# Sliding-window attention into a gated feed-forward layer: another order for the tail rows' loads, the first score tiles, batch 1's steps, the later q and k jobs and the last output tile

## The chip, the cores and the metric

The kernel runs on one core of one Trainium2 chip. The time is the device time of one execution in microseconds (us); five executions of the kernel before gave 329.77, 330.66, 330.7, 331.74 and 332.5, and their median, 330.7 us, is the number to compare with. One execution was also recorded by the hardware profiler. It is the one of 331.74 us; the recorded span, from the first to the last instruction, is 330.0 us of it, and 1.7 us lie around the span. All instants below are us from the start of that span.

The engines are called PE (TensorE, the matrix engine; PEld is its weight load), ACT (ScalarE), DVE (VectorE), POOL (GpSimd) and SP (SyncE, which here only issues transfers).

## The reference, cut to what matters

```python
# q, k, v: 8 batches x 8 heads x 576 rows x 64, float32
scores = q @ k.T / 8
rel = pos[:, None] - pos[None, :]
mask = (rel >= 0) & (rel < 128)                 # each row sees itself and 127 rows before it
scores = where(mask, scores - slope[h] * abs(rel), -1e9)
attn = softmax(scores, axis=-1)
x = (attn @ v) put together to 4608 tokens x 512
h = x @ w_in                                    # 512 -> 2048
g = h * sigmoid(beta * h)
out = g @ w_out                                 # 2048 -> 512, float32
```

Attention is small and banded: a block of 128 keys meets only its own block of query rows and the next one. The two dense products of the second half are large: 4608 x 512 x 2048 each.

## The kernel before, in words

**Tiling.** A batch has 576 = 4 x 128 + 64 rows; the last 64 rows are its tail. Heads go in pairs p = 0..3. `SC(b, m, p)` makes a score tile of a pair, transposed (keys on the partitions): m = 0 holds key blocks 0 and 1, m = 1 holds key blocks 2, 3 and 4, of which block 4 is the tail. Its matmuls are at L285; in batches 0 and 1 two matmuls at L271 add the bias first and one ACT exponential follows (L293); in later batches four ACT exponentials (L298) and a DVE mask (L302) follow. `PV(b, qb, g)` multiplies the exponentials of four heads with v (L325, L329), and DVE divides by the row sums (L334, L335). `X(b, qb)` brings the result to the layout that the dense half reads, `XT`: for batches 0 to 2 by four PE transposes and a copy out of PSUM (L358; ACT for batches 0 and 2, DVE for batch 1), from batch 3 on by a transposing transfer from SP (L349). `HS(g, j)` is one of 16 slices of the first dense product for a group g of 512 tokens: four matmuls (L372), a tanh on ACT (L377) and a multiply on DVE into `gT` (L378). `OS(g, i, n)` is a quarter of the second product for 128 tokens (four matmuls, L388; quarter n reads slices 4n to 4n+3 of `gT`); after n = 3 the tile is scaled and stored. There are nine groups.

**How q, k and v come in.** All loads from DRAM are f32. For batches 0 to 2, `load_pair(b, p)` loads 512 rows of q and of k of two heads in runs of 1024 bytes (L109), and POOL casts them to bf16 (L113). `load_tail(b)` loads the tails of all heads in runs of 256 bytes (L95), and POOL casts them (L119). PE transposes them, `TP(b, p, i)` (i = 0 for q, 1 for k; L224) and `TT(b)` for the tail (L238), and ACT or DVE copies the result to `QK[b % 2]` (L229, L243). From batch 3 on, `load_qk(b, sb)` loads a block of 128 rows of q and of k in runs of 256 bytes (L95), POOL casts both (L129), and `TD(b, sb)` issues two transposing transfers from SP into `QK` (L248), one for q and one for k. v is loaded by SP and cast by POOL (L142) for batches 0 to 2, and loaded with a cast by POOL's own queue later (L137). W_in comes in four POOL transfers (L188) and W_out in four (L191), some of them tied to follow a certain cast.

**What sets the order.** PE's order is the program's order, written by hand. For SP and POOL this holds as well from the line with `steps, first = ...` on (L657): `merge` puts jobs (loads, casts, transposing transfers) between the attention steps by a due step. `first[b]` is the step at which batch b's scores begin: 26 for batch 3, 47 for batch 4, 70, 93 and 116 for the others. A q, k job of block sb is due at `first[b] - 25 + 4.6 * sb`, its cast 4.5 steps later and its `TD` 8.5 steps later. SP and POOL run their lists strictly in order; SP waits where a cast isn't done. `spread(moe, todo, lead, goals)` mixes dense items with attention steps: after each dense item it runs as many steps as the sum of their costs (1 or 2 each) allows, on a straight line that begins after `lead` items.

**PSUM.** Transposes, `PV` and `X` of batches 0 to 2 share two buffers (`psum_t`, tag "t"). `HS` has two. In batch 1 score tiles alternate between `psum_s` and `psum_y`, one buffer each.

**Batches 0 and 1 and the end.** Batch 0's steps are a written list (L586 to L609); batch 1's are `by_pair(1)`, seven `HS` items of group 0 between them (L640). The last group's items at L672 are 16 `HS` with the 13 open `OS` of the group before between the first 13 of them; then 16 `OS` follow at L685.

Of the kernel before, what the change touches and what calls it, by code (L numbers as in the profile page):

```python
# [17 lines left out]
def kernel(  # L18
# [98 lines left out]
    def load_tail(b):  # L117
        for i, src in enumerate((q, k)):
            nc.gpsimd.tensor_copy(  # L119
                out=tails[b % 2][0 : S - LM, i], in_=load_rows(src, b, NQB - 1)  # L120
            )
# [37 lines left out]
        nc.gpsimd.memset(VS[i][64:P, 4, :, :], 0.0)  # L159
        nc.gpsimd.memset(VS[i][:, :, :, D : D + 1], 1.0)  # L160
    nc.scalar.dma_start(out=bflat[:], in_=moe_beta.rearrange("(j p) -> j p", p=P))
    load_pair(0, 0)
    load_pair(0, 1)
    load_tail(0)
    load_pair(0, 2)
    load_pair(0, 3)
    for h in range(H):
        nc.scalar.mul(sident[:, h, :], ident[:], slopes[h] / qscale)

# [171 lines left out]
    def X(b, qb):  # L341
        nq = ROWS[qb]
        xnv = xns.pop((b, qb))[:].rearrange("p h d -> p (h d)")
        tok0 = (b * S + P * qb) % XTR
        n1 = min(nq, XTR - tok0)
        parts = [(tok0, 0, n1)] + ([(0, n1, nq)] if n1 < nq else [])
        if b >= NTE:
            for at, r0, r1 in parts:
                nc.sync.dma_start_transpose(out=XT[:, :, at : at + r1 - r0], in_=xnv[r0:r1, :])  # L349
            return  # L350
        xt = psum_t.tile([P, NDM, P], BF16, name="xt", tag="t")
        for c in range(NDM):
            nc.tensor.transpose(
                out=xt[:, c, :], in_=xnv[:, c * P : (c + 1) * P], identity=ident[:]
            )
        copy = nc.vector.tensor_copy if b == 1 else nc.scalar.copy
        for at, r0, r1 in parts:
            copy(out=XT[:, :, at : at + r1 - r0], in_=xt[:, :, r0:r1])  # L358

# [64 lines left out]

    cost = {}

    def spread(moe, todo, lead, goals):
        sums = [0]  # L430
        for f in todo:
            sums.append(sums[-1] + cost.get(f, 0))
        goals = [(m, sums[n]) for m, n in goals]
        m0, w0, k = lead, 0, 0
        slope = None
        for i, it in enumerate(moe):
            flush()
            it()
            while goals and (slope is None or i + 1 >= m1):

                if slope is not None:
                    m0, w0 = m1, w1
                    goals = [g for g in goals if g[0] > m0]
                    if not goals:
                        break
                slope, m1, w1 = max(((w - w0) / (m - m0), m, w) for m, w in goals)
            w = w0 + slope * (i + 1 - m0)
            while k < len(todo) and (sums[k] + sums[k + 1]) / 2 <= min(w, w1):
                todo[k]()
                k += 1  # L450
        for f in todo[k:]:
            f()

    def step(f, c):
        cost[f] = c
        return f

    def tp(b, p, i):
        return step(lambda: TP(b, p, i), 1)

    def tt(b):
        return step(lambda: TT(b), 1)

    def sc(b, m, p):
        def f():
            pool = None
            if "y" in spare:
                pool = spare["y"][0]
                spare["y"].reverse()
            SC(b, m, p, pool)  # L470

        return step(f, 2)

    def pv(b, qb, g):
        return step(lambda: PV(b, qb, g), 1)

    def x(b, qb):
        f = step(lambda: X(b, qb), int(b < NTE))
        at[b, qb] = f
        if b >= NTE:  # L480
            lazy.append(f)
        return f
# [5 lines left out]
    def merge(steps, first):  # L488
        jobs = []

        def vals(b, sb, t0):
            casts = []
            jobs.append((t0, lambda: casts.append(load_v(b, sb))))
            if b < NTE:
                jobs.append((t0 + 4.5, lambda: casts.pop()()))

        for sb in range(NQB):
            vals(NTE - 1, sb, 1.5 * sb)
        for b in range(NTE, B):
            for sb in range(NQB):  # L500
                casts = []
                t0 = first[b] - 25 + 4.6 * sb
                jobs.append((t0, lambda b=b, sb=sb, c=casts: c.append(load_qk(b, sb))))
                jobs.append((t0 + 4.5, lambda c=casts: c.pop()()))
                jobs.append((t0 + 8.5, lambda b=b, sb=sb: TD(b, sb)))
                vals(b, sb, first[b] - 16 + 3 * sb)
        for i, f in enumerate(steps):
            if f in lazy:
                jobs.append((i + 2, f))
        jobs.sort(key=lambda j: j[0])  # L510
        out = []
        for i, f in enumerate(steps):
            while jobs and jobs[0][0] <= i:
                out.append(jobs.pop(0)[1])
            if f not in lazy:
                out.append(f)
        return out + [j[1] for j in jobs]

    def by_pair(b):
        return [  # L520
            tp(b, 0, 0), tp(b, 0, 1), tp(b, 1, 0), sc(b, 0, 0), tp(b, 1, 1), tp(b, 2, 0),
            sc(b, 0, 1), tp(b, 2, 1), tp(b, 3, 0), sc(b, 0, 2), tp(b, 3, 1), tt(b), pv(b, 0, 0),
            sc(b, 0, 3), pv(b, 1, 0), sc(b, 1, 0), pv(b, 0, 1), sc(b, 1, 1), pv(b, 1, 1),
            sc(b, 1, 2), x(b, 0), pv(b, 2, 0), sc(b, 1, 3), x(b, 1), pv(b, 3, 0), pv(b, 4, 0),
            pv(b, 2, 1),
        ]
# [30 lines left out]
    with tc.manual_schedule(engines={mybir.EngineType.PE}):  # L557
# [7 lines left out]
        for p in range(NP):  # L565
            c = load_pair(1, p, None if p else VS[0][0:1, NQB - 1, 0, 0:1])
            if p == 1:
                with tc.issue_after(c.ins):
                    load_w1(3)
                load_tail(1)  # L570
        for sb in range(NQB):
            c = load_v(1, sb)()
            if sb == 3:
# [3 lines left out]
        with tc.tile_pool(name="psum_x", bufs=2, space=bass.MemoryType.PSUM) as psum_x:  # L577
            pools = [psum_x, psum_s, psum_x]

            def sc0(m, p, fill=0):  # L580
                SC(0, m, p, pools[0], fill)
                pools.append(pools.pop(0))

            w = psum_t.tile([P, 512], F32, name="w", tag="t")
            idle(w[:], 9)
            TP(0, 0, 0)  # L586
            c = TP(0, 0, 1)
            with tc.issue_after(c.ins):
                late_consts()
            sc0(0, 0, 3)  # L590
            load_beta()
            TP(0, 1, 0)
            TP(0, 1, 1)
            sc0(0, 1, 2)
            TT(0)
            TP(0, 2, 0)
            sc0(1, 0, 1)
            TP(0, 2, 1)
            sc0(1, 1)
            TP(0, 3, 0)  # L600
            sc0(0, 2)
            TP(0, 3, 1)
            sc0(1, 2)
            PV(0, 0, 0)
            sc0(0, 3)
            PV(0, 1, 0)
            sc0(1, 3)
            for qb in (2, 3):
                PV(0, qb, 0)  # L609
# [22 lines left out]
            del spare["z"]  # L632
        for p in range(NP):
            load_pair(2, p)
            if p == 1:
                load_tail(2)

        with tc.tile_pool(name="psum_y", bufs=1, space=bass.MemoryType.PSUM) as psum_y:
            spare["y"] = [psum_s, psum_y]
            spread(h0[7:14], s1[2:-1], 0, [(7, len(s1) - 3)])  # L640
            del spare["y"]
        psum_o = ctx.enter_context(
            tc.tile_pool(name="psum_o", bufs=2, space=bass.MemoryType.PSUM))
# [13 lines left out]
        with tc.manual_schedule(engines={mybir.EngineType.SP, mybir.EngineType.Pool}):  # L657


            order = [(i, n) for i in range(4) for n in range(4)]  # L660

            def os(g, order):
                return [lambda i=i, n=n: OS(g, i, n) for i, n in order]

            todo = [[]]
            for f in merge(steps, first):
                if f in visits:
                    todo.append([])
                todo[-1].append(f)
            moe = [hs(1) + os(0, order[0:12]), os(0, order[12:]), os(1, order[0:3])]  # L670
            for g in range(2, NTG):
                o = os(g - 1, order[3:]) + (os(g, order[0:3]) if g < NTG - 1 else [])  # L672
                for j, h in enumerate(hs(g)):
                    moe[-1].append(h)
                    if j % 4 == 1:
                        moe.append([])
                    moe[-1] += o[j : j + 1]
            for n, m in enumerate(moe):
                r = todo[n] if n < len(todo) else []
                if n and r:  # L680
                    r.pop(0)()
                spread(m, r, 2 if n == 0 else 1, [(len(m) - (n == 0), len(r))])
            while stores:
                flush()
            for it in os(NTG - 1, order):  # L685
                it()


# [28 lines left out]
```

## Time and profile before

| quantity | value |
|---|---|
| median of five executions | 330.7 us |
| the profiled execution, and its span | 331.74 us, 330.0 us |
| PE busy | 313.8 us (95%) |
| ACT, DVE, POOL busy | 214.9, 190.7, 107.1 us |
| granted PE clock | full in every slice (only the first nine warm-up matmuls of 512 columns come 0.43 us apart, later ones 0.213 us) |
| q, k and v transfers issued by SP, median time to landing | 4.9 to 6.4 us |
| transposing transfers L248, median time to landing | 4.0 us |

PE's busy time counts every matmul to its modelled end, so a dense stretch reads as full. Where PE stands still it shows in the list of PE's waits, which names the instruction that waited and what released it. A transfer has two instants: the issue on its queue (SPq or POOLq rows) and the landing, after which its reader may start.

### The profile page before, as it was taken

The numbers are of one execution on the slowest core, as the hardware profiler recorded it, in microseconds if no ns is written. First come the engines' busy times: TensorE is split into PE (matmuls) and PEld (weight loads), VectorE is DVE, ScalarE is ACT, GpSimd is POOL, SyncE is SP. The second block draws the span as 40 slices with busy tenths as digits, with TensorE's granted clock in tenths as the row PEclk, the third lists the DMA queues.
The fourth block names the chain that finished last, engine by engine and source line by source line (L and its number), as shares of the span: only waits on it lengthen the run. The fifth ranks groups of instructions, "written<-read, shape, count | busy, mean of one in ns | idle before, by whom it ended". The sixth has DMA issues, their size and how long they took to land.

```text
span 330.0 us, 6155 instructions
## 1 busy us (share of the span) xinstructions
PE 313.8 (95%) x2238; PEld 154.0 (47%) x2280; DVE 190.7 (58%) x413; ACT 214.9 (65%) x416; POOL 107.1 (32%) x173
## 2 busy tenths in 40 slices
PE   8979798999998999999999999999999999999995
PEld 3444345544544544454445444444444444444442
DVE  7658458995445666666666666666665434433400
ACT  5757684887786777777777777777764444544411
POOL 7743583166553443433344235300000000010000
PEclk9999999999999999999999999999999999999999
DMA  7999999999999999999999899921122200001011
GB/s 183 257 186 253 223 231 237 187 203 184 203 208 180 185 217 174 189 186 201 176 171 184 159 193 193 176 64 51 48 71 68 57 32 32 32 34 64 33 66 64
DMA packets 138638, 48.26 MB, mean 146 GB/s; under 512 B 125664, under 2 KB 136176, under 8 KB 138608
## 3 DMA queue, kind: packets, MB, share of 16 engines
q1 hardware_dynamic: 108208, 32.19, 54.0%
q0 software_dynamic: 30224, 15.54, 30.9%
q8 instruction: 18, 0.29, 0.4%
q10 hardware_dynamic: 176, 0.14, 0.1%
q14 instruction: 12, 0.10, 0.1%
HBM read 36.71 MB, written 9.44 MB: 140 GB/s over the span
## 4 chain that ended last, share of the span: by engine, by line
PE 65%; DMA 21%; SPq 5%; POOL 2%; issue 2%; ACT 2%; DVE 1%; POOLq 0%
PE ops L388 32%; PE hps L372 27%; DMA fst<-in_v_dram 8%; DMA fst<-in_k_dram 7%; DMA fst<-in_q_dram 4%; PE sps L285 3%; SPq L248 2%; PE pv L329 2%; SPq L95 2%; PE pv L325 1%; DMA qkT<-bst 1%; SPq L109 1%; ACT pt L298 1%; POOL vs L142 1%; DVE gT L378 1%
## 5 line engine op out<-in xcount | busy, mean ns | idle before, releaser
L377 ACT ACTIVATE sig<-hps,beta_h 128x512 bf16<-128x512 f32 x144 | 99.8, 696 | 79.4 <-PE hps L372 60.9
L372 PE MATMUL hps<-XT,W 128*128 128x512 bf16 x554 | 144.1, 379 | 2.6 <-ACT XT L358 0.7
L388 PE MATMUL ops<-W,gT 128*128 128x512 bf16 x559 | 143.2, 379 | 1.4 <-issue 0.2
L378 DVE SCALAR_TENSOR_TENSOR gT<-sig,hps 128x512 bf16<-128x512 bf16 x144 | 98.3, 684 | 66.8 <-ACT sig L377 66.5
L388 PEld LDWEIGHTS <-gT 128*128 128x128 bf16 x576 | 53.9, 98 | 64.1 <-issue 2.1
L372 PEld LDWEIGHTS <-W 128*128 128x128 bf16 x576 | 51.1, 97 | 52.4 <-issue 3.8
L298 ACT ACTIVATE pt<-sps,bias 128x256 bf16<-128x256 f32 (+1 forms) x192 | 73.0, 494 | 3.7 <-PE sps L285 3.7
L129 POOL CAST bst<-fst 128x512 bf16<-128x512 f32 (+1 forms) x50 | 32.4, 650 | 77.2 <-DMA fst<-in_q_dram 60.8
L302 DVE TENSOR_TENSOR pt<-pt,mask 128x1024 bf16<-128x1024 bf16 x48 | 34.1, 711 | 36.2 <-ACT pt L298 36.1
L406 POOL DMA_DIRECT2D out_dram<-osb x32 | 17.9, 559 | 91.2 <-ACT osb L403 91.1
L335 DVE TENSOR_TENSOR xn<-pv,zs 128x256 bf16<-128x256 f32 (+1 forms) x80 | 33.7, 422 | 2.5
L403 ACT ACTIVATE osb<-ops 128x512 f32<-128x512 f32 x35 | 20.9, 598 | 15.3 <-PE ops L388 15.3
L329 PE MATMUL pv<-vs,pt 128*128 128x65 bf16 x320 | 28.6, 193 | 1.6 <-POOL vs L142 1.1
L329 PEld LDWEIGHTS <-pt 128*128 128x128 bf16 x320 | 21.7, 97 | 10.6 <-issue 0.8
L325 PE MATMUL pv<-vs,pt 128*128 128x65 bf16 x256 | 24.1, 193 | 0.7 <-DVE XT L358 0.5
L325 PEld LDWEIGHTS <-pt 128*128 128x128 bf16 x256 | 19.9, 98 | 8.0 <-issue 1.6
L285 PE MATMUL sps<-qkT 64*128 64x256 bf16 (+2 forms) x320 | 21.9, 251 | 1.5 <-DMA qkT<-bst 1.4
L137 POOL DMA_DIRECT2D vs<-in_v_dram x25 | 21.4, 855 | 0.6 <-issue 0.5
L285 PEld LDWEIGHTS <-qkT 64*128 64x128 bf16 x320 | 11.2, 94 | 20.5 <-issue 15.7
L113 POOL CAST bst<-fst 128x512 bf16<-128x512 f32 x24 | 14.6, 623 | 17.6 <-DMA fst<-in_q_dram 12.9
L334 DVE RECIPROCAL zs<-pv 128x4 f32<-128x4 f32 (+1 forms) x80 | 14.0, 176 | 10.9 <-PE pv L329 10.7
L293 ACT ACTIVATE pt<-sps 128x1024 bf16<-128x1024 f32 x16 | 16.4, 1024 | 6.0 <-PE sps L285 5.3
(49 smaller groups left out, 109.6 us busy)
## 6 DMA issues: line engine op xcount, KB each, us to landing
fst<-in_q_dram SPq DMA_DIRECT2D x32, 256.0 KB, 4.9
fst<-in_k_dram SPq DMA_DIRECT2D x32, 256.0 KB, 5.2
out_dram<-osb POOLq DMA_DIRECT2D x32, 256.0 KB, 3.6
fst<-in_v_dram SPq DMA_DIRECT2D x12, 256.0 KB, 6.4
vs<-in_v_dram POOLq DMA_DIRECT2D x20, 128.0 KB, 5.3
W<-in_moe_w_in_dram POOLq DMA_DIRECT2D x4, 512.0 KB, 7.2
W<-in_moe_w_out_dram POOLq DMA_DIRECT2D x4, 512.0 KB, 15.3
fst<-in_q_dram SPq DMA_DIRECT2D x8, 128.0 KB, 5.0
```

The costliest lines, as they stand in the source:

```text
L129: nc.gpsimd.tensor_copy(out=t[0 : ROWS[sb], i], in_=f)
L137: nc.gpsimd.dma_start(out=to, in_=v[b, :, P * sb : P * sb + ROWS[sb], :].rearrange("h p d -> p h d"))
L285: nc.tensor.matmul(o, lhsT=qk[64 * e : 64 * e + 64, 1, p, P * kb : P * kb + P], rhs=qk[64 * e : 64 * e + 64, 0, p, P * kb : P * kb + nq], ...
L298: nc.scalar.activation(out=pt[:, e, cols], in_=sps[e][:, cols], func=ACTF.Exp, scale=qscale, bias=bias[:, half, h : h + 1],)
L302: nc.vector.tensor_tensor(out=pt[:], in0=pt[:], in1=masks[m][:].rearrange("p (o c) -> p o c", o=1).broadcast_to([P, 2, 512]), op=ALU.mult,)
L325: nc.tensor.matmul(pv[:, hl, 0 : D + 1], lhsT=weights(b, qb - 1, h, 1), rhs=vs[:, qb - 1, h, 0 : D + 1], start=True, stop=False,)
L329: nc.tensor.matmul(pv[:, hl, 0 : D + 1], lhsT=weights(b, qb, h, 0), rhs=vs[:, qb, h, 0 : D + 1], start=qb == 0, stop=True,)
L335: nc.vector.tensor_tensor(out=xn[0:nq, 4 * g : 4 * g + 4, :], in0=pv[0:nq, :, 0:D], in1=zs[0:nq].broadcast_to([nq, 4, D]), op=ALU.mult,)
L372: nc.tensor.matmul(hps[:], lhsT=W1[:, c, bass.ts(j, P)], rhs=XT[:, c, c0 : c0 + TOKG], start=(c == 0), stop=(c == NDM - 1),)
L377: nc.scalar.activation(out=sig[:], in_=hps[:], func=ACTF.Tanh, scale=beta_h[:, j : j + 1])
L378: nc.vector.scalar_tensor_tensor(out=gts[g][:, j, :], in0=sig[:], scalar=1.0, in1=hps[:], op0=ALU.add, op1=ALU.mult)
L388: nc.tensor.matmul(ops_[:], lhsT=gT[:, j, i * P : i * P + P], rhs=W2[:, j, :], start=(j == 0), stop=(j == NFF - 1),)
```

## The change

Six edits. (1) In all of batches 0, 1 and 2 the tail's two loads and casts go behind the four pairs, where they stood between pairs 1 and 2. (2) In batch 0 the copies of `X` alternate between ACT (row blocks 0, 2, 4) and DVE (1, 3). (3) Batch 0's list makes the m = 0 tiles of all four pairs first, then the tail's transposes, then the m = 1 tiles. (4) Batch 1 gets a list of its own, in which score tiles come two at a time; `spread` runs the second of such a pair at once, and its `lead` for batch 1 is 1 in place of 0. (5) From batch 3 on a q, k job is due at `first[b] - 27.5 + 4.2 * sb`: 2.5 steps sooner for block 0 and 4.1 for block 4, with its cast and its `TD`. v's jobs keep their steps. (6) The first three quarters `OS(8, 0, 0..2)` of the last group stand behind its last three `HS` items, one behind each, as in the other groups.

```diff
-    load_pair(0, 0)
-    load_pair(0, 1)
+    for p in range(NP):
+        load_pair(0, p)
     load_tail(0)
-    load_pair(0, 2)
-    load_pair(0, 3)
...
-        copy = nc.vector.tensor_copy if b == 1 else nc.scalar.copy
+        copy = nc.vector.tensor_copy if b == 1 or b == 0 and qb % 2 else nc.scalar.copy
...
-    cost = {}
+    cost, second = {}, []
...
-            while k < len(todo) and (sums[k] + sums[k + 1]) / 2 <= min(w, w1):
+            while k < len(todo) and (
+                (sums[k] + sums[k + 1]) / 2 <= min(w, w1) or todo[k] in second
+            ):
...
+        if b == 1 and p % 2:
+            second.append(f)
         return step(f, 2)
...
-                t0 = first[b] - 25 + 4.6 * sb
+                t0 = first[b] - 27.5 + 4.2 * sb
...
     def by_pair(b):
+        if b == 1:
+
+            return [
+                tp(b, 0, 0), tp(b, 0, 1), tp(b, 1, 0), tp(b, 1, 1), tp(b, 2, 0), sc(b, 0, 0),
+                sc(b, 0, 1), tp(b, 2, 1), tp(b, 3, 0), tp(b, 3, 1), tt(b), sc(b, 0, 2),
+                sc(b, 0, 3), pv(b, 0, 0), pv(b, 1, 0), sc(b, 1, 0), sc(b, 1, 1), pv(b, 0, 1),
+                pv(b, 1, 1), sc(b, 1, 2), sc(b, 1, 3), x(b, 0), pv(b, 2, 0), x(b, 1),
+                pv(b, 3, 0), pv(b, 4, 0), pv(b, 2, 1),
+            ]
...
-                load_tail(1)
+        load_tail(1)
...
+            TP(0, 2, 0)
+            TP(0, 2, 1)
+            sc0(0, 2, 2)
+            TP(0, 3, 0)
+            TP(0, 3, 1)
+            sc0(0, 3)
             TT(0)
-            TP(0, 2, 0)
-            sc0(1, 0, 1)
-            TP(0, 2, 1)
+            sc0(1, 0)
             sc0(1, 1)
-            TP(0, 3, 0)
-            sc0(0, 2)
-            TP(0, 3, 1)
+            PV(0, 0, 0)
             sc0(1, 2)
-            PV(0, 0, 0)
-            sc0(0, 3)
             PV(0, 1, 0)
             sc0(1, 3)
...
-            if p == 1:
-                load_tail(2)
+        load_tail(2)
...
-            spread(h0[7:14], s1[2:-1], 0, [(7, len(s1) - 3)])
+            spread(h0[7:14], s1[2:-1], 1, [(7, len(s1) - 3)])
...
-                o = os(g - 1, order[3:]) + (os(g, order[0:3]) if g < NTG - 1 else [])
+                o = os(g - 1, order[3:]) + os(g, order[0:3])
...
-            for it in os(NTG - 1, order):
+            for it in os(NTG - 1, order[3:]):
```

## The prediction

> **What bounds the kernel now.** I read the page first (busy shares and the 40 slices):
>
> ```profile
> PE 313.8 (95%) x2238; PEld 154.0 (47%) x2280; DVE 190.7 (58%) x413; ACT 214.9 (65%) x416; POOL 107.1 (32%) x173
> ...
> PE   8979798999998999999999999999999999999995
> ...
> DMA  7999999999999999999999899921122200001011
> ```
>
> PE is the bound from about 100 us on, and no edit removes PE work, so only PE's pauses can be won: slices 1 to 7 and one later. The DMA row is full for two thirds of the span: early, a transfer's place in line matters as much as PE's order. PE's waits over the whole span, second:
>
> ```profile
> PE tps L224 <- POOL bst L113: 2.0, 1, 2.0
> PE sps L285 <- DMA qkT<-bst: 1.4, 1, 1.4
> ...
> PE pv L329 <- POOL vs L142: 1.1, 1, 1.1
> PE hps L372 <- ACT XT L358: 0.7, 1, 0.7
> PE hps L372 <- DVE gT L378: 0.6, 1, 0.6
> ```
>
> Each is one event. PE's timeline places them at 32.8, 98.5, 17.6, 22.4 and 310.5. Counted from matmul start to start, less the 0.213 us that a 512-column matmul takes in dense stretches, the second is 1.54 and the last 0.80. The third view is the chain of waits around the second:
>
> ```profile
> 93.51 0.62 POOL bst L129
> 94.14 1.30 SPq L248
> ...
> 95.53 4.31 DMA qkT<-bst
> ...
> 99.89 0.51 PE sps L285 x10
> ```
>
> PE reached SC(3,1,0) at 98.23 and stood until the k half of TD(3,4) landed at 99.84. Is that a late issue, or a full DMA? The DMA view of 64 to 100 us in 40 slices:
>
> ```profile
> DMA  6388999999999999929999999999999159999996
> ```
>
> Full, but for the start and two gaps. So TD(3,4) lands when the work ahead of it is through. That work starts with W_in, W_out and batches 1 and 2's loads, gated by v casts, not by PE's progress. It follows that PE's clock is reset at 99.84: whatever edits 1 to 4 win before that is spent waiting there, and whatever they lose is forgiven up to 1.5 us. This is the core of the forecast.
>
> [...] v's POOL load issued at 94.62 lands at 99.64, between the two halves of TD(3,4) (99.04 and 99.84). [...] batch 0's pairs (1024-byte runs) land 0.7 to 0.8 us apart, its tails, half the bytes in 256-byte runs, 0.9 us. [...]
>
> **Edits 1, 2, 3: batch 0.** PE's wait at 17.6 ends with v block 3's cast (18.00 to 18.62), whose load lands at 17.95. The ten q, k loads before it are the same, in another order, so the cast stays. New order up to there: pair 2's casts come about 1 us sooner, pair 3's end at 11.1 (12.7 before), the tail's at 12.7. With 0.69 us per DVE copy the m = 0 tiles end near 14.1, TT near 14.6, and four m = 1 tiles of 0.95 us with two PVs near 18.3: 0.3 us before v. Nothing won; the one more filler matmul (0.2 us) is hidden by that wait, and costs itself if v comes sooner. X's four ACT copies take 20.47 to 23.0 in a row. With two on DVE (0.42 us) block 1's copy stands ahead of block 3's reciprocal and multiply (0.18 and 0.42), so the last copy ends at 23.0 to 23.3: 0 to +0.2.
>
> **Edits 1, 4: batch 1.** TP(1,2,0) waits because POOL casts the tail first:
>
> ```profile
> 33.01 1.18 POOL L119 CAST tail<-fst 64x512 bf16<-64x512 f32 x2
> 34.12 1.17 POOL L113 CAST bst<-fst 128x512 bf16<-128x512 f32 x2
> ...
> 34.79 0.40 PE L224 MATMUL tps<-ident,bst 128*128 128x128 bf16 x4 [2.00 <-POOL bst L113]
> ```
>
> With the tail last, pair 2's q is cast from 33.01 to 33.63 and PE goes on at 33.7: 1.1 us won. What is late next: three TPs and TT now follow one another on two PSUM buffers. The third waits for the ACT copy of the first, which stands behind an exponential (1.02) and a tanh (0.69): about 1.1 us lost near 37; before, TT and PV lost 0.7 there. After h13, x, pv, x, pv, pv, pv come in a row on the same buffers; DVE's copies (0.42) and pairs (0.6) pace them as they did (0.67 + 0.32). By this count h14 comes at 51.1, before 51.2. It rests on DVE taking what is ready first, as at 44.43, where a reciprocal precedes the gT of an earlier slice; in strict program order I get 53.5. So PE's shift at 54 us lies between -0.2 and +2.3, and I take -0.1. All of it meets 99.84.
>
> **Edit 5: batch 3.** With the due steps written out, SP's list up to TD(3,4) holds the same transfers in both kernels (five v, seven q, k pairs, eight TDs); only the pairs of blocks 2, 3, 4 each move ahead of one TD. The same issues, the same bytes: no gain from SP. On POOL, v block 0 of batch 4 (step 31) stood ahead of the casts of q, k block 1 (31.1), now behind them (28.2). Those casts end at 98.1, so that load, which occupied the DMA from 97.5 to 99.3, drops behind TD(3,4). Its price is the spacing of such loads, 1.0 to 1.3 us. Bounds: 0, if the DMA fills otherwise, to 1.6, from where TD(3,4)'s own least time to landing (2.5 us, the shortest of any L248) binds. I take 1.1: PE goes on at 98.8 in place of 99.89, **-1.1**. On the way, SC(3,0,0) at 86.62 needs TD(3,2)'s q half (landed 86.19). It is now behind block 4's pair (0.66 + 0.69 of SP, 1.3 us of DMA), but ahead of two v loads that follow later casts (-2.6 us of DMA); SP's issue then binds, 86 to 87: at most 0.4 us, forgiven at 98.8. v and k casts of batch 2 swap places by two casts (1.2 us); PV(2,0,0) runs at 71, 4 us after v's cast.
>
> **Edit 5: batch 4.** The next first score tile and the transfer it needs, from the timelines of PE and SP:
>
> ```profile
> 115.88 0.61 PE L285 MATMUL sps<-qkT 64*128 64x256 bf16 x8
> ```
>
> ```profile
> 106.66 4.19 SPq L248 DMA_TRANSPOSE qkT<-bst  x2
> ```
>
> TD(4,2)'s q half took 7.8 us to land, at 114.5: 1.4 us of slack. PE now arrives at 114.8. SP's list before TD(4,2) gets block 4's pair in addition: 0.63 + 0.62 us of issue, 1.3 us of DMA; against that the DMA's empty slice near 106 (0.8 us). I get 115.0, bounds 113.5 and 118.4: **+0.3**. Batches 5 to 7 have slack of 3.3 to 5.2 us, and XT is read some 30 us after it lands.
>
> **Edit 6: the end.**
>
> ```profile
> 308.64 1.89 PE L372 MATMUL hps<-XT,W 128*128 128x512 bf16 x8
> ...
> 311.16 1.02 PE L372 MATMUL hps<-XT,W 128*128 128x512 bf16 x4 [0.63 <-DVE gT L378]
> ```
>
> Three HS in a row on two PSUM buffers lose 0.80. With an OS between (0.86 us) each buffer has 1.73 us and the loss goes, as in the earlier rows. But OS(8,0,3) now follows h15 by one OS. h15 starts at 312.1, its gT is ready 2.55 us later (1.06 to tanh, 0.72, 0.72), at 314.65; the fourth matmul of that OS would come at 314.45. Loss 0.2 (bounds 0 and 0.9, if the whole OS waits). **-0.6.**
>
> **Sum.** -1.1 + 0.3 - 0.6 = -1.4: the profiled execution goes from 331.74 to 330.3. The median shown is 330.7, 1.0 lower; I take the same difference: 329.3 us.
>
> **Rivals.** (a) TD(3,4) lands where it did, since the order of the same bytes moves nothing, or batch 1 loses 2.3 us and PE itself comes at 100: only the end is won, -0.6 to -0.5, 330.1. For it: the equal lists. Against: v's load ahead of it. (b) The DMA gains more, because casts done sooner let SP issue TDs without a pause (it waited 4.0 us on L129 casts from 75 to 105), and PE's early gain counts: -1.5 - 0.5 - 0.6 = -2.6, 328.1. Against: those pauses were filled by DMA work. (c) Slower: TD(4,2) becomes the bound. Batch 4's first v loads, dropped behind TD(3,4), fall into its way (two of 1.3 us) with block 4's pair (1.3): it lands at 118.4, PE waits 3.6 us: -1.1 + 3.6 - 0.6 = +1.9, 332.6. It decides from a landing after 116.5 on, 2.0 us later than before.
>
> **How the numbers follow.** A measurement of this kernel can tell about 0.5%, 1.65 us: faster is below 329.05, slower above 332.35. My forecast (own range 328.5 to 330.1) gets 0.45, of which 0.2 is faster; (b) 0.20, faster; (a) 0.20, of which 0.02 faster, the rest same; (c) 0.15, slower. That makes 0.42, 0.43 and 0.15. The range 327.8 to 332.0 leaves out the far ends of (b) and most of (c).
>
> **What would show it.** Right: PE's wait on the tps of pair 2 falls from 2.0 to about 1; a wait on qkT stays near 98 us, ended by TD(3,4), although PE came there at its time or sooner; batch 4's first score tile waits little; no HS wait at 310, a short OS wait at 314. Wrong: no wait on qkT at all with PE ahead by over 2 us; waits on qkT near 86 or 115 of over 1 us; new waits near 50 us of over 2 us in all.

## The result, and the profile after

The change makes the kernel slower. The median is 335.67 us over 44 executions, against 331.64 us over 79 executions of the kernel before on the same chips. The ratio is 1.0067, with a 95% interval from 1.0050 to 1.0085; it compares the executions of each kernel that lie within 1.5% of its own fastest, which is why it is smaller than the quotient of the medians, 1.0122. The prediction, 329.3 us and most likely faster or equal, was wrong.

The profiled execution of the kernel after took 338.19 us (span 336.2 us), one of the longer ones. Its main losses are named below and looked for again in the experiments. In the kernel after, most line numbers are two lower than before: L370 and L386 are the matmuls of `HS` and `OS` (before L372, L388), L283 those of the score tiles, L246 `TD` and L347 `X`. From the page, its span and the rows of PE and of PE's granted clock in the 40 slices (8.4 us each):

```profile
span 336.2 us, 6162 instructions
...
PE   7889888999799995999999999999999999999995
...
PEclk9999999999999999799999999999999999999999
```

PE has a hole in slice 16, which is 126 to 134 us, and the clock a dent right behind it, in slice 17. Before, neither row showed anything there. PE's waits over the whole span, the longest two and the one that edit 1 was aimed at:

```profile
PE hps L370 <- DMA XT<-xn: 3.4, 1, 3.4
PE sps L283 <- DMA qkT<-bst: 1.7, 1, 1.7
...
PE tps L222 <- POOL bst L113: 0.2, 1, 0.2
```

The wait on `tps` fell from 2.0 to 0.2 us. The wait on `qkT` is at 87.7 us now, in batch 3's first score tile (before it was at 98.5, in its second). The wait on `XT` is new, and the largest of all. PE's timeline around it, after:

```profile
129.43 1.03 PE L386 MATMUL ops<-W,gT 128*128 128x512 bf16 x4
133.85 1.26 PE L370 MATMUL hps<-XT,W 128*128 128x512 bf16 x4 [3.39 <-DMA XT<-xn]
134.90 1.91 PE L386 MATMUL ops<-W,gT 128*128 128x512 bf16 x4
```

HS(3,0), the first slice of group 3, cannot start before X(3,2), the transposing transfer of batch 3's third row block, has landed at 133.80. The four matmuls behind it take 1.26 and 1.91 us, where four take 1.03 at the full clock. The SP queue shows why X(3,2) is late. First the kernel before, then the kernel after; the columns are start, duration of the issue, queue, line, operation (x2 stands for two transfers; the first of the last row is X(3,2)):

```profile
122.99 0.57 SPq L95 DMA_DIRECT2D fst<-in_q_dram  x1
123.61 1.27 SPq L95 DMA_DIRECT2D fst<-in_k_dram  x1
124.98 1.66 SPq L349 DMA_TRANSPOSE XT<-xn  x1
126.74 2.51 SPq L248 DMA_TRANSPOSE qkT<-bst  x2
```

```profile
124.05 1.02 SPq L95 DMA_DIRECT2D fst<-in_q_dram  x1
125.11 1.50 SPq L95 DMA_DIRECT2D fst<-in_k_dram  x1
126.72 3.38 SPq L246 DMA_TRANSPOSE qkT<-bst  x2
130.20 2.53 SPq L347 DMA_TRANSPOSE XT<-xn  x2
```

X(3,2) has step 52 in both lists. Before, the transfers of TD(5,0) were due at 53.5 and the q, k pair of batch 5's block 2 at 54.2, both behind it. Edit 5 makes them due at 51.0 and 50.9, ahead of it. They hold SP from 124.05 to 130.10 without a pause, so X(3,2) is issued at 130.20 instead of 124.98, and lands at 133.80 instead of 129.35.

Counted at PE's first weight load of a slice, after minus before: HS(1,0) +0.75; HS(2,0) +2.48, through the new wait of 1.7 at 87.7; HS(2,8) +1.02, as the old wait of 1.5 at 98 is gone; HS(3,0) +4.43; HS(3,8) +6.15; the last `OS` +6.28. So the whole is 1.02 up to the middle of group 2, 3.41 for X(3,2), 1.72 from the reduced clock after it, 0.76 around one short wait on a `gT` near 209 us that no other profile here shows, and -0.63 at the end (edit 6): together 6.28. This is the sum for one pair of profiles; the first of these terms lies within the scatter that profiles of one order show below.

### The profile page after: what moved, and what is told of

Its sections match the earlier page's. It is cut to its first block, busy times and chain, and to the rows that moved or that the text cites. A ratio compares the mean times of both kernels' runs of the same rounds, so it can differ in the third digit from the quotient of the medians.

```text
span 336.2 us, 6162 instructions
## 1 busy us (share of the span) xinstructions
PE 315.9 (94%) x2238; PEld 154.3 (46%) x2281; DVE 192.2 (57%) x415; ACT 212.8 (63%) x414; POOL 107.1 (32%) x173
## 4 chain that ended last, share of the span: by engine, by line
PE 78%; DVE 7%; ACT 6%; DMA 5%; issue 2%; SPq 1%; POOL 0%
PE hps L370 33%; PE ops L386 31%; PE sps L283 4%; ACT pt L296 3%; PE pv L327 2%; DVE gT L376 2%; PE pv L323 2%; DMA qkT<-bst 2%; ACT sig L375 2%; DMA fst<-in_q_dram 2%; PE sps L269 2%; DVE qkT L227 1%; PE tps L222 1%; PE w L211 1%; DVE xn L333 1%
## 5 line engine op out<-in xcount | busy, mean ns | idle before, releaser
L370 PE MATMUL hps<-XT,W 128*128 128x512 bf16 x552 | 144.9, 380 | 6.2 <-DMA XT<-xn 3.4
L386 PE MATMUL ops<-W,gT 128*128 128x512 bf16 x562 | 144.8, 381 | 1.0
L386 PEld LDWEIGHTS <-gT 128*128 128x128 bf16 x576 | 53.9, 98 | 64.7 <-issue 2.9
L370 PEld LDWEIGHTS <-W 128*128 128x128 bf16 x576 | 51.1, 98 | 57.3 <-issue 5.0
L300 DVE TENSOR_TENSOR pt<-pt,mask 128x1024 bf16<-128x1024 bf16 x48 | 34.9, 727 | 37.0 <-ACT pt L296 36.9
L283 PE MATMUL sps<-qkT 64*128 64x256 bf16 (+2 forms) x320 | 21.9, 251 | 3.0 <-DMA qkT<-bst 1.7
L283 PEld LDWEIGHTS <-qkT 64*128 64x128 bf16 x320 | 11.2, 94 | 22.1 <-issue 17.6
L291 ACT ACTIVATE pt<-sps 128x1024 bf16<-128x1024 f32 x16 | 15.7, 1022 | 8.4 <-PE sps L283 8.3
```

The lines of the kernel that those rows point to most:

```text
L283: nc.tensor.matmul(o, lhsT=qk[64 * e : 64 * e + 64, 1, p, P * kb : P * kb + P], rhs=qk[64 * e : 64 * e + 64, 0, p, P * kb : P * kb + nq], ...
L300: nc.vector.tensor_tensor(out=pt[:], in0=pt[:], in1=masks[m][:].rearrange("p (o c) -> p o c", o=1).broadcast_to([P, 2, 512]), op=ALU.mult,)
L370: nc.tensor.matmul(hps[:], lhsT=W1[:, c, bass.ts(j, P)], rhs=XT[:, c, c0 : c0 + TOKG], start=(c == 0), stop=(c == NDM - 1),)
L386: nc.tensor.matmul(ops_[:], lhsT=gT[:, j, i * P : i * P + P], rhs=W2[:, j, :], start=(j == 0), stop=(j == NFF - 1),)
```

## The experiments

Each was timed next to the kernel before. Ratios are to that kernel, with 95% intervals. The columns of instants are of one profiled execution each: PE's first weight load for HS(0,4), HS(1,0) and HS(3,0), the landing of X(3,2), and the weight load of the last `OS` (us).

| | kernel | ratio | HS(0,4) | HS(1,0) | X(3,2) lands | HS(3,0) | last OS |
|---|---|---|---|---|---|---|---|
| | before | | 27.16 | 54.63 | 129.35 | 129.41 | 325.40 |
| | after | 1.0067 [1.0050, 1.0085] | 27.72 | 55.39 | 133.80 | 133.84 | 331.68 |
| 1 | after, X(3,2) ahead | 0.9977 [0.9963, 0.9991] | 27.95 | 55.62 | 126.51 | 128.71 | 324.12 |
| 2 | before + edit 5 | 1.0093 [1.0063, 1.0124] | 27.26 | 55.42 | 133.36 | 133.40 | 331.04 |
| 3 | before, X(3,2) late | 1.0169 [1.0136, 1.0202] | 27.57 | 54.07 | 132.21 | 132.25 | 329.78 |
| 4 | after without edit 5 | 0.9965 [0.9947, 0.9983] | 27.48 | 55.14 | 129.14 | 129.20 | 324.45 |
| 5 | after, fillers in the wait | 1.0080 [1.0057, 1.0102] | 27.55 | 55.22 | 132.71 | 132.50 | 328.21 |
| 6 | 1, and TDs ahead of loads | 0.9975 [0.9958, 0.9993] | 28.14 | 55.81 | 127.23 | 128.92 | 324.40 |
| 7 | before + 5 + 6, X(3,2) ahead | 0.9961 [0.9938, 0.9984] | 27.92 | 55.29 | 128.09 | 128.46 | 324.05 |
| 8 | before + edit 6 | 0.9976 [0.9956, 0.9996] | 27.25 | 54.42 | 128.62 | 128.68 | 323.91 |
| 9 | 1 without edit 4 | 0.9942 [0.9914, 0.9969] | 27.96 | 54.61 | 129.61 | 129.72 | 324.92 |
| 10 | before + edit 1, batches 1, 2 | 0.9969 [0.9950, 0.9988] | 26.68 | 53.75 | 127.92 | 127.98 | 323.93 |
| 11 | 7 + edit 1, batches 1, 2 | 0.9914 [0.9877, 0.9950] | 26.87 | 53.52 | 128.09 | 128.71 | 324.61 |

In run 5 HS(3,0)'s weights were loaded under the fillers; its matmuls started at 132.75.

### 1. The kernel after, with X(3,2) put back ahead of the jobs

```diff
-                jobs.append((i + 2, f))
+                jobs.append((i + (0.5 if f is at[NTE, 2] else 2), f))
```

> The changed kernel, with one transfer moved: X(3,2), the layout transfer of batch 3's third row block, is due 1.5 steps sooner, so that SP issues it ahead of the q, k loads of block 2 and the TD of block 0 of batch 5, as before the change, where it stood behind them. Theory (that place in SP's list made the 3.4 us wait of the first dense item of group 3): it lands near 128 to 129.5 us, the wait falls under 0.5 us, PE keeps its full clock, and the kernel ends 3.5 to 6 us sooner than the changed kernel: within 1 us of the kernel before. Rival (the transfers are in all too many by then, any order is late): it lands after 132, and a wait of 2.5 us or more stays. Second rival (the half clock at 134 to 138 us is a state of the machine, not an effect of the wait): the clock drops in this kernel as often as in the changed one.

This line is the only difference to the kernel after, and it turns 1.0067 into 0.9977: 0.9% or 3.0 us. (Of the medians of all executions, the quotient goes from 1.0122 to 0.9962.) SP's queue now reads:

```profile
120.05 3.11 SPq L347 DMA_TRANSPOSE XT<-xn  x2
123.22 0.58 SPq L95 DMA_DIRECT2D fst<-in_q_dram  x1
123.84 1.33 SPq L95 DMA_DIRECT2D fst<-in_k_dram  x1
125.29 2.81 SPq L246 DMA_TRANSPOSE qkT<-bst  x2
```

X(3,1) and X(3,2) go first and the pair and TD(5,0) behind them. X(3,2) lands at 126.51, sooner than the 128 to 129.5 expected, and PE reads it at 128.71; no wait on `XT` is left. There is no wait on a TD either, at 87 us included; that one is not the edit's doing, as section 4 says. (The margin is not the same in each kernel: in run 9 X(3,2) is ahead as well, but lands at 129.61, and PE stands 0.99 us.)

### 2. Edit 5 alone

```diff
-                t0 = first[b] - 25 + 4.6 * sb
+                t0 = first[b] - 27.5 + 4.2 * sb
```

> The kernel before with edit 5 alone (q, k jobs of batches 3 to 7 sooner). Theory: it brings both losses by itself: a wait of 2 to 3 us on TD(3,2) near 87 us (PE comes there 0.75 us sooner than in the changed kernel), none on TD(3,4), a wait of 3 to 4 us on X(3,2) near 130 us, and the half clock after it in part of the executions: 3 to 7 us slower than before, at least as slow as the changed kernel less its win at the end (0.6). Rival (the losses need edits 1 to 4, which shift PE against the transfers): no wait over 1 us at 130, within 1 us of before.

The loss comes back without the other five edits. PE's waits:

```profile
PE hps L372 <- DMA XT<-xn: 3.9, 1, 3.9
```

The stop of 2 to 3 us that was expected at TD(3,2) did not come: its q half landed at 87.05 and PE did not wait for it. So the stop at 87.7 in the kernel after is no fixed part of edit 5.

### 3. X(3,2) late in the kernel before

```diff
-                jobs.append((i + 2, f))
+                jobs.append((i + (4.3 if f is at[NTE, 2] else 2), f))
```

> The kernel before with X(3,2) alone moved behind the TD of block 0 and the q, k loads of block 2 of batch 5; nothing else is sooner or later. Theory: TD pair and loads take 3.8 us of SP, so it lands near 133 us in place of 129.4, the first dense item of group 3 waits 3.4 to 4 us[...]: 3.5 to 6 us slower than before. The wait of 1.4 us on TD(3,4) stays. Rival (the place of X(3,2) is not what counts): within 1 us of before.

No q, k job moves; X(3,2) alone is put behind TD(5,0) and the pair. That is enough:

```profile
PE hps L372 <- DMA XT<-xn: 3.6, 1, 3.6
```

Runs 1 to 3 settle the cause from both sides: the order of X(3,2) against TD(5,0) and one pair makes the loss, in either kernel, and the order alone takes it away. Why run 3's ratio is above run 2's, with a shorter stop in its profile, no run shows.

### 4. The kernel after without edit 5

```diff
-                t0 = first[b] - 27.5 + 4.2 * sb
+                t0 = first[b] - 25 + 4.6 * sb
```

> The changed kernel with edit 5 undone (the due steps of the q, k jobs as before): edits 1, 2, 3, 4 and 6. Theory: PE comes to TD(3,4) 0.75 us later than before and waits 0.7 in place of 1.4 us, so nothing is lost there; the end wins 0.6; X(3,2) is where it was: 0.3 to 1 us faster than the kernel before. Rival (batch 1's list costs more than the wait on TD(3,4) forgives): slower than before by 0.5 us or more.

0.9965: without edit 5 the change is a gain. Next to run 1 (0.9977) it also says that edit 5 with X(3,2) ahead wins nothing measurable over edit 5 left out; runs 7 (0.9961) and 8 (0.9976), the same pair without edits 1 to 4, differ as little.

The wait of 0.7 us on TD(3,4) that was expected is not in this profile. How much such a wait depends on the execution is shown by profiles that have the same order up to there. Run 8 is the kernel before up to the last group, run 3 up to 120 us: PE waits 1.4 us for TD(3,4) in the kernel before, 1.2 us in run 3 and not at all in run 8, where it landed at 97.97 in place of 99.84. With edit 5, the kernel after and runs 1 and 5 have one order up to 115 us: PE waits 1.7, 0 and 1.3 us for TD(3,2), which landed at 89.34, 86.30 and 88.73. A wait of this size in one profile is not yet a property of the order.

### 5. The same wait, filled with matmuls

The fillers are 14 matmuls of zeros into the tile that HS(3,0) then overwrites, so PE is busy while X(3,2) is on its way. They add work and change no result.

```diff
         hps = pool.tile([P, TOKG], F32, name="hps", tag=tag)
+        if g == 3 and j == 0:
+            idle(hps[:], 14)
```

> The changed kernel with 14 filler matmuls of 512 columns (3.0 us) in front of the first dense item of group 3, where PE stood idle for 3.4 us; the filler multiplies zeros into the item's own PSUM tile, which the item then starts afresh. Theory (the half clock at 134 to 138 us comes from that idle stretch): PE waits for X(3,2) no less, the item's first matmul is at the same time within 1 us, but the clock stays full, and the kernel ends 1.5 to 2.5 us sooner than the executions of the changed kernel that had the half clock: 3 to 4.5 us slower than before. Rival (the clock drop is a state of the machine, or comes of something else): the same drop, the same time as the changed kernel or later.

What PE does in the kernel after between 130 and 138 us, and in this one. The columns are the stretch, its length, busy time of PE, PEld, DVE, ACT and POOL with the number of instructions, PE's clock, the DMA's share and GB/s. After:

```profile
130.00:132.00 2.00, 0.45 (x3) 0.00 (x0) 1.30 (x4) 0.32 (x1) 1.57 (x3) 1.00 1.53 166
132.00:134.00 2.00, 0.15 (x1) 0.11 (x2) 0.00 (x0) 0.00 (x0) 0.91 (x1) 1.00 1.32 258
134.00:136.00 2.00, 2.00 (x7) 0.77 (x6) 0.14 (x1) 0.69 (x1) 0.00 (x0) 0.63 1.00 166
136.00:138.00 2.00, 2.00 (x13) 0.99 (x12) 1.14 (x3) 0.60 (x1) 0.35 (x1) 0.52 1.75 217
```

With fillers, the clock in the two stretches after the wait, and PE's timeline (the fillers add two lines, so that L372 is `HS` again):

```profile
134.00:136.00 2.00, 2.00 (x23) 1.05 (x23) 1.19 (x3) 1.31 (x3) 0.00 (x0) 1.00 1.45 148
136.00:138.00 2.00, 2.00 (x17) 0.94 (x14) 0.72 (x2) 2.00 (x6) 0.01 (x1) 1.00 1.45 227
```

```profile
129.70 3.19 PE L211 MATMUL hps<-zero 128*128 128x512 bf16 x14
132.75 1.02 PE L372 MATMUL hps<-XT,W 128*128 128x512 bf16 x4
```

X(3,2) lands as late as in the kernel after (132.71), but the clock stays at 1.00 and PE's delay against before does not grow afterwards: +3.1 at HS(3,0), +3.3 at HS(3,8). In the kernel after it grew from 4.43 to 6.15 in the same stretch, in runs 2 and 3 from 4.00 to 5.53 and from 2.84 to 4.37. So in these three profiles stops of 3.4, 3.9 and 3.6 us each cost another 1.5 to 1.7 us at a reduced clock. In the kernel after the clock is 1.00 from 133.80 to 134.50, with HS(3,0) already running, 0.50 over the whole of 134.55 to 137.90, and 1.00 from 137.95 to 140: 3.4 us at half. In each of the three profiles the stretches of 2 us with a clock below 1.00 lack 1.7 us of clock in all (in the kernel after 0.37 of one and 0.48 of the other); if it was at 0.50 in runs 2 and 3 too while it was low, that makes 3.4 us there as well, an estimate. The kernel before stood 2.0 us at 33 us, and its clock is 1.00 from 28 to 40 us in that profile. How long a stop has to be to cost the clock, no run shows.

The six executions with fillers lie between 334.48 and 335.12 us (median 334.81), all at a clock of 0.999 or more. Those of the kernel after spread from 330.91 to 338.56: 27 of 44 have a mean clock below 0.997 (median 336.84), the other 17 a median of 333.20. So the fillers win 2.0 us against the first and lose 1.6 against the others, which is why the ratio, 1.0080, is no better than 1.0067. The spread would fit a stop that is shorter in some executions, or one of the same length that does not always cost the clock; there is no profile that would tell.

### 6. TD ahead of the loads

```diff
-                jobs.append((t0 + 8.5, lambda b=b, sb=sb: TD(b, sb)))
+                jobs.append((t0 + 8.3, lambda b=b, sb=sb: TD(b, sb)))
```

> X(3,2) sooner as in the first experiment, and each TD due 0.2 steps sooner (8.3 in place of 8.5), which puts it ahead of the q, k loads two blocks later, as before the change, where the new spacing of 4.2 had put it behind them. If these swaps cost anything (the wait of 1.7 us on TD(3,2) in the changed kernel's profile), this is up to 0.5 us faster than the first experiment and TD(3,2) and TD(4,2) land 1 us sooner; if the DMA sets the landing and not SP's list, it is the same within 0.3%.

Run on top of run 1, it changes which of a TD and a load pair with nearly the same due step goes first. TD(3,2)'s q half lands at 85.22 (86.30 in run 1), TD(4,2)'s at 111.40 (111.01), and the time is the same (0.9975 against 0.9977). PE waits for neither in either profile: with that slack, these swaps cost and win nothing that shows.

### 7 and 8. Edits 5 and 6 with X(3,2) ahead, and edit 6 alone

```diff
-                o = os(g - 1, order[3:]) + (os(g, order[0:3]) if g < NTG - 1 else [])
+                o = os(g - 1, order[3:]) + os(g, order[0:3])
...
-            for it in os(NTG - 1, order):
+            for it in os(NTG - 1, order[3:]):
```

> The kernel before with edits 5 and 6 and X(3,2) due 1.5 steps sooner: the first experiment without edits 1 to 4. Theory: edits 1 to 4 only shift PE by +0.5 to +1 us at 54 us, and with TD(3,4) landing at 96 to 99 nothing forgives that any more. So this is 0.3 to 1 us faster than the first experiment and 1.5 to 2.5 us faster than before (the wait on TD(3,4) 1.4, the end 0.6). Rival (edits 1 to 4 win something): 0.5 us or more slower than the first experiment.

> The kernel before with edit 6 alone: the last group's first three quarters behind its last three dense items. Expected: the wait of 0.6 us near 310 us goes, a wait of about 0.2 us at the fourth quarter comes (bounds 0 and 0.9), 0.6 us or 0.2% faster than before; if the whole fourth quarter waited for the last dense item, no gain.

Run 8 is the diff above on the kernel before; run 7 has the diffs of runs 1 and 2 besides. Edit 6 alone gives 0.9976, that is 0.8 us, interval 0.1 to 1.5. The `HS` wait at 310 is gone in every kernel that has it. In run 7 PE waits for nothing over 0.1 us on a transfer after 80 us. It was expected 1.5 to 2.5 us faster than before and came 1.3 us faster (interval 0.5 to 2.1); that it beats run 1 by 0.3 us or more isn't shown, since the intervals overlap.

### 9 to 11. Which of edits 1 to 4 costs what

Run 9 is run 1 with `by_pair(1)`, `spread`'s rule and `lead` as before. Run 10 is the kernel before with this:

```diff
-            if p == 1:
-                load_tail(2)
+        load_tail(2)
```

and the same for batch 1; batch 0 keeps its order. Run 11 has this and run 7's diffs.

> The kernel after with X's transfer first (as in the first experiment) and without edit 4: batch 1 takes its steps in the order of before, while its tail is loaded last. Theory: edits 1 to 4 cost about 0.6 us at 54 us, and it is the list of batch 1 (edit 4) that costs it; then PE comes to the first slice of group 1 at about 54.8 in place of 55.6, the ratio is 0.995 to 0.997, and there is a wait on the tail's transposes of at most 0.5 us, since the old order asks for the tail after pair 3. Rival: the loss is that of edits 1 to 3 (the tail's place and batch 0's list); then 54 us shows the same +0.8 as before and the ratio stays at 0.9977.

> The kernel before with edit 1 in batches 1 and 2 alone (batch 0 is left). The prediction's step: the wait on pair 2's tile falls from 2.0 us to about 1, and all of that is lost again by 100 us, where PE waits for TD(3,4): ratio 0.998 to 1.001. Rival: with that 2 us pause gone, the kernel holds the full clock in all its executions (before shows a mean clock below 0.9965 in about 4 of 10); then at most 1 in 20 of its executions shows a lower clock, and the ratio stays within 0.998 to 1.001 all the same.

> Before with edit 1 in batches 1 and 2, edit 5, edit 6, and the third X transfer of batch 3 ahead of the jobs: no edit of batch 0's order and of batch 1's list. Theory: the gains of the end (0.6 us), of TD(3,4) (1.1) and of the pause at pair 2 (up to 1) add up, since nothing makes PE wait at 98 us any more: ratio 0.992 to 0.995, last OS at 323.2 or sooner in the profile. Rival: what is won at pair 2 is lost in batch 1's remaining steps: 0.996, as without edit 1.

Take three groups of profiles from the table: those without edits 1 to 4 (before, 2, 3, 7, 8), those with all four (after, 1, 4, 5, 6), and runs 9 to 11.

They are single profiles, and PE has the same order in the whole first group up to HS(1,0): the range from 54.07 to 55.42 us there is scatter from execution to execution. So the sizes that follow are estimates.

*Batch 0 (edits 1 to 3).* HS(0,4) comes at 27.80 on average in the six profiles that have them (27.48 to 28.14, with run 9), at 27.24 in the seven that don't (26.68 to 27.92), and at 27.43 in the five of these that have none of edits 1 to 4: about 0.4 to 0.6 us lost.

*Edit 1 in batches 1 and 2.* From HS(0,4) to HS(1,0) the kernels without edits 1 to 4 take 26.50 to 28.16 us, mean 27.33; runs 10 and 11 take 27.07 and 26.65. That is 0.5 us less on average, but within the spread; what speaks for a gain is run 10's ratio, 0.9969. PE's timeline of run 10, where before had one wait of 2.00:

```profile
32.24 0.40 PE L224 MATMUL tps<-ident,bst 128*128 128x128 bf16 x4 [0.46 <-POOL bst L113]
33.54 0.40 PE L224 MATMUL tps<-ident,bst 128*128 128x128 bf16 x4 [0.90 <-POOL bst L113]
```

*Edit 4.* The same stretch takes 27.66 or 27.67 in all five kernels with batch 1's own list, and 26.65 in run 9, which differs from run 1 by that list alone: 1.0 us lost, by this one profile. The ratios point the same way (0.9942 against 0.9977), though their intervals just overlap and the chips differ. PE's timeline after shows three of the pieces:

```profile
38.50 0.38 PE L222 MATMUL tps<-ident,bst 128*128 128x128 bf16 x4 [0.80 <-ACT qkT L227]
...
50.55 0.20 PE L323 MATMUL pv<-vs,pt 128*128 128x65 bf16 x1 [0.71 <-DVE xn L333]
...
51.70 0.20 PE L323 MATMUL pv<-vs,pt 128*128 128x65 bf16 x1 [0.42 <-DVE xn L333]
```

The first is the third transposition in a row on two PSUM buffers, the others are PVs in a row on the same two buffers, each waiting until DVE has emptied the one two places ahead.

At HS(1,0) the group with all four edits stands at 55.44 on average and the group without at 54.77, +0.7. The three pieces add to +0.9 to +1.1, as near as this scatter allows.

Run 11 is the best of all: 0.9914, 2.9 us below the kernel before, interval 1.7 to 4.1. It has neither batch 0's order nor batch 1's list. Run 9's interval overlaps its own, and run 7, without edit 1, was timed on another chip, so that edit 1 adds to run 7 is likely but not shown. Its profiled execution is one of its longer ones. There PE comes 1.1 us sooner to HS(1,0) and is stopped at 85.9 by TD(3,2):

```profile
87.32 0.50 PE L285 MATMUL sps<-qkT 64*128 64x256 bf16 x6 [1.47 <-DMA qkT<-bst]
```

So what is won early isn't always kept, and the last `OS` at 324.61 misses the 323.2 of the theory in this profile; what is next to be moved is TD(3,2). Run 10's ratio is better than its theory gave: PE stood only 0.8 us for TD(3,4), which landed at 98.67, so at most part of the gain at pair 2 was lost there, and "forgiven" is too strong a word for that stop as well. Run 9 came near its theory: 54.61 at HS(1,0) for about 54.8, and 0.9942 for 0.995 to 0.997.

One thing stays open. In the executions of the kernel before that were made for these runs, 55 of 141 have a mean clock below 0.9965 although no profile of it shows where; run 7 has 7 of 21 and run 8 has 6 of 22. Kernels with edits 1 to 4 and X(3,2) in time have 1 of 66 (runs 1, 4, 6), run 9 none of 17, run 10 3 of 22, run 11 none of 8. The stop of the kernel before at 33 us, 2.0 us, is at most 0.9 us in all of the latter. Run 10 shortens it and does nothing else, but 3 of 22 next to 12 of 40 of the kernel before beside it is more than the 1 in 20 expected, and too few to decide. X(3,2) does not explain it: run 7 has it ahead, run 4 where before has it.

## Why the prediction was wrong, and where it was right

**The step that failed.** "Batches 5 to 7 have slack of 3.3 to 5.2 us, and XT is read some 30 us after it lands." This clause priced edit 5's effect on X's transfers at nothing, and it is false for one of them. X(3,2) landed at 129.35 in the kernel before and PE loaded HS(3,0)'s weights at 129.41. The same 0.06 us stand between the two in runs 4, 8 and 10, which have X(3,2) where before has it. The matmuls themselves waited for a second thing, the PSUM buffer of HS(2,14), which DVE had read by 129.54 in the kernel before. The chain of waits of before, which names DVE alone:

```profile
128.93 0.61 DVE gT L378
129.54 0.04 issue
129.58 1.02 PE hps L372 x4
```

So X(3,2) had 0.2 us to spare, and not 30: whatever delayed it by more was paid for in full. Over the 26 transfers of `X` of batches 3 to 7 the time from landing to the first weight load of the group that reads it goes from 0.06 to 43 us in the kernel before, and only 8 have 30 us or more. In run 8 that buffer was free at 127.54, PE was there sooner, and stood; PE's timeline:

```profile
128.71 1.02 PE L372 MATMUL hps<-XT,W 128*128 128x512 bf16 x4 [0.94 <-DVE gT L378]
```

The releaser named is DVE, whose `gT` of HS(2,15) ended at 128.66, but that belongs to the other buffer (in run 4 HS(3,0) starts 0.6 us before it ends); what HS(3,0) waited for was X(3,2), landed at 128.62. The trace of before held both numbers of the 0.06 us. The step compared positions in SP's list up to TD(4,2) and then stopped; X(3,2) is issued 18 us later in the same list, and a pair and TD(5,0) had moved past it. They took 6.05 us of SP, and the landing came 4.45 us later. None of the rivals had this mechanism; rival (c) was the right sort of loss (a transfer pushed behind moved jobs) at the wrong transfer.

**The term that had no place in the sum.** In the three profiles with a stop of 3.4 to 3.9 us the clock went down after it (to 0.50 for 3.4 us in the kernel after), which cost another 1.5 to 1.7 us. A price for a wait of this length has to include it.

**"PE's clock is reset at 99.84."** By this the prediction meant PE's place in time, and called it the core of the forecast. It was a reading of one execution. Runs 3, 4, 8 and 10 have TD(3,4) where before has it, and it lands at 99.09, 98.37, 97.97 and 98.67; PE waits 1.2, 0, 0 and 0.8 us. There is no fixed instant at which early gains and losses end.

**Edit 5, batch 3: -1.1.** Not shown as a gain. TD(3,4) lands between 97.97 and 99.84 in the five profiled kernels without edit 5 (mean 98.8) and between 95.58 and 99.35 in the eight with it (mean 97.8): the size of the step, within a spread that is larger. (The least time to landing of an L248, put at 2.5 us in the bound, is 2.4.) That v's load, which landed at 99.64 in the kernel before, cost TD(3,4) 1.1 us was an estimate from the spacing of such loads; no run moves that load alone. And "forgiven at 98.8" failed on the way. TD(3,2)'s q half was put at most 0.4 us late; it lands at 85.00 to 86.19 without edit 5 (mean 85.6) and at 86.30 to 89.34 with it (mean 87.7, run 6 left out). In the kernel after that is a stop of 1.7 us at 87.7. There it took the place of the stop at 98, so that the wait moved and little was won: 4 against 1, and 8 against 7, are equal within their intervals.

**Edit 5, batch 4: +0.3.** Right in effect: no wait there over 0.7 us in any profile, TD(4,2)'s q half at 113.56 in the kernel after against the predicted 115.0.

**Edits 1 to 3, batch 0: 0 to +0.2.** Too low; about +0.4 to +0.6. The count followed PE and v's cast and left out ACT. Its timeline, the exponentials of batch 0, before and then after:

```profile
11.90 6.38 ACT L293 ACTIVATE pt<-sps 128x1024 bf16<-128x1024 f32 x6 [0.73 <-PE sps L285]
```

```profile
12.23 1.02 ACT L291 ACTIVATE pt<-sps 128x1024 bf16<-128x1024 f32 x1 [1.08 <-PE sps L283]
14.34 1.02 ACT L291 ACTIVATE pt<-sps 128x1024 bf16<-128x1024 f32 x1 [1.08 <-PE sps L283]
15.69 3.99 ACT L291 ACTIVATE pt<-sps 128x1024 bf16<-128x1024 f32 x4 [0.34 <-PE sps L283]
```

Before, m = 1 tiles filled the time until the next pair was transposed, and ACT ran six in a row, to 18.28. With the m = 0 tiles first, ACT stands twice for 1.08 us until the next pair arrives, and ends at 19.68. PE's m = 1 tiles ended near 18.5, as counted (18.3), but PE then waits for that last exponential (0.40 us before a filler matmul), not for v. (The spacing of 0.7 to 0.8 us that the prediction gives for the pairs' landings is right for three of them; pair 1's q and k land at 6.39 and 7.43, 1.04 us apart.)

**Edits 1, 4: -0.2 to +2.3, taken -0.1.** Inside the bounds, with about +0.3 between HS(0,4) and HS(1,0); the value taken was somewhat too good. The slice h14 came at 51.93 in the kernel after, not 51.1; run 9, without the list, has 51.16. The gain at pair 2 and the loss at the third transposition were both seen (the latter put at 1.1, measured 0.80); of the PVs near 50 us the count said that DVE's work would "pace them as they did", and they cost 0.71 and 0.42 us. That DVE takes what is ready first was the author's estimate from one place, 44.43; no run shows it as a rule.

**Edit 6: -0.6.** Right: -0.63 between the profiles, and 0.8 us in the timing of run 8. The `HS` wait at 310 went as said, and the loss at the `OS` near 314 is 0.16 us in runs 1, 4, 7, 8, 9 and 11 (0.2 predicted).

**The signs named.** The `tps` wait fell, to 0.2 rather than to about 1. "Waits on qkT near 86 or 115 of over 1 us" was named as what would make the prediction wrong, and the first came true. A wait near 98 us, named as a sign of being right, is gone. No sign was named for `XT`.

## What to carry to other kernels

When jobs move forward in an in-order queue, list every entry that they pass, to the end of the list, with the time from its landing to its first reader; a reader that starts at the moment of landing (here 0.06 us after it) has next to no slack even if no wait is shown. Moving a job sooner wins nothing where nobody waits for it, and what it passes may pay. Before a wait in one profile is counted as something to win, see whether a second profile of the same order has it. And price a stop of the matrix engine as long as those here, 3.4 to 3.9 us, with the clock that it may lose, 1.5 to 1.7 us here.

## What the runs showed of the hardware

In three profiles (the kernel after, runs 2 and 3) a stop of PE of 3.4 to 3.9 us was followed by stretches of 2 us with a clock of 0.50 to 0.86, for 1.5 to 1.7 us of lost time; in the kernel after it was 0.50 for 3.4 us. With 14 matmuls of zeros (3.19 us) in the same place, in run 5, it was 1.00 in every stretch from 126 to 140 us. Issuing from SP takes time that counts: in the lists above, where the DMA row of the page stands at 9, a TD's pair of transfers held the queue for 2.5 to 3.4 us, two loads 1.8 to 2.5 us.
